# One core, attention and two MLPs: the written-out order of 1,198 steps is replaced by another order of the same steps

## The chip, the cores and the metric

The kernel runs on one core of a Trainium2 chip. The metric is the device time of one execution in microseconds (us). Lower is better. The engines are named as in the profile: PE is the matrix engine, PEld its weight loads, DVE the vector engine, ACT the scalar engine, POOL the GpSimd engine, and SP the queue that issues all loads and stores here.

## The reference

```python
# attention: q, k, v are (2, 8, 576, 64)
q_d = q.reshape(B, H, 144, 4, D).mean(axis=3)      # k_d, v_d alike
out_d = softmax_attention(q_d, k_d, v_d)           # scale 1/sqrt(D)
out_up = np.repeat(out_d, 4, axis=2)
mask = np.abs(pos[:, None] - pos[None, :]) < 4
out_local = softmax(where(mask, scale * q @ k.T, -1e9)) @ v
x = (out_up + out_local) -> (1152, 512)
# first MLP: w_in (512, 2048), w_out (2048, 512)
h = x @ w_in
x = where(h > 0, h, exp(min(h, 0)) - 1) @ w_out
# second MLP: 4 experts, w1 (512, 1024), w2 (1024, 512) each
p = probs / (probs.sum(-1) + 1e-9)
out = sum_e p[:, e] * (maximum(x @ w1[e], 0) @ w2[e])
```

The inputs of the first MLP's weights are 64-bit numbers, which the kernel converts itself from their two 32-bit words.

## The kernel before, in words

All products of the MLPs are done in three passes on numbers that are split into a high and a low part, so that a product step of the first MLP is 12 matmuls of 288 columns.

The attention and the first MLP are not a loop nest. They are cut into steps, and a string, `ORDER`, lists them. `run` takes the string token by token and issues each step's instructions. From then on nothing reorders them: each engine executes its own instructions in the order of the string, and an instruction that waits for another engine holds up all that stands behind it on its own engine. After the string comes the second MLP (`quad`, `l2e`), whose order a program merges; the change doesn't touch it.

A token is a name, its indices, and behind a colon an option: `:v`, `:a` or `:g` chooses DVE, ACT or POOL, and a number chooses how many products of nothing PE executes first. Those are matmuls of the identity with a column of zeros, 256 columns wide, into the step's own PSUM bank, which the step's real matmuls then overwrite (line 480). There are eight PSUM banks in a ring: a step that takes one waits until the step that held it has been read out.

The digit 0 or 1 in front of an attention step is the batch. The steps that the change and the prediction speak of:

- `LK`, `LV`, `VB`, `wF`, `mF`, `nF`: loads on the SP queue (queries and keys, values, slices of values, weights).
- `CP`: copies a loaded half of q or k into another layout (batch 0 only). `Tp`: PE transposes it (line 575). `Te`: DVE or ACT moves the result from PSUM to `qkT`.
- `PQ`: DVE sums `qkT` over groups of four into `pooled` (line 592). `PVa`, `PVb`: the same for v, on POOL.
- Local attention, nine blocks a batch: `LSp` scores (lines 621 and 625), `LSm` maximum (DVE, line 634), `LSx` exponentials (ACT), `LEr` and `LEm` normalise (line 661), `LTp` transposes (line 669), `LTe` moves, `LPp` multiplies by v (line 685), `LPa` adds the pooled part, `LPh` and `LPl` write the high and the low part of x (line 710).
- Pooled attention: `GSp` scores (line 722), `GSm`, `GSx`, `GEr`, `GEm` (line 764) the softmax, `GTp` transposes (line 776), `GTe` moves, `GPp` and `GPe` the product with v (line 799).
- Weights of the first MLP, in eight pieces a slice: `wA` (ACT), `wB`, `wC` (line 302), `wD` (line 309), `wE` (line 316) on DVE convert; `wH` (ACT) and `wL` (line 330, DVE or POOL) split.
- First MLP: `hp` product (line 264, `psH`), `ha`, `he` (ACT), `hd` (DVE), `hh` (ACT), `hl` (line 866, DVE or POOL); then `yp` product (line 264, `psY`) and `ya`, which adds it up.
- `m` and `n` steps prepare the first weights of the second MLP, and `xh`, `xl`, `xd`, `xth`, `xtl` its input. `W` is ten products of nothing at the start, and `C` closes the attention's memory.

Loaded tensors and split weights share nine slots of memory (`s8`). A load waits until the tensor that had its slot was used up, and loads behind it on SP wait too.

Of the kernel before, what the change touches and what calls it, by code (L numbers as in the profile page):

```python
# [1125 lines left out]
```

## Time and profile before

| | us |
|---|---|
| median of 3 runs | 672.08 |
| lowest and highest run | 671.48 and 673.28 |
| profiled execution | 674.41 |
| its span, from the first to the last instruction | 672.2 |

The profiled execution's time has 2.2 us outside its span. Its mean granted PE clock is 1.000. Busy times are from this one execution. A share of busy time is a mean over stages: the attention and the first MLP end at about 292 us of the span, and the second MLP takes the rest.

### The profile page before, as it was taken

How to read it: one execution, taken by the hardware profiler on the slowest of the kernel's cores; microseconds unless marked ns; L12 is line 12 of the kernel's file. 1: busy time of each engine (PE TensorE's matmuls, PEld its weight loads, DVE VectorE, ACT ScalarE, POOL GpSimd, SP SyncE). 2: the span in 40 equal slices, each digit the busy share in tenths (PEclk: the TensorE clock that was granted, in tenths of full speed). 3: DMA queues.
4: the chain of work that ended last, by engine and by line, in shares of the span. 5: the costliest groups of instructions: out<-in, count | busy, mean ns of one | idle time of the engine just before them, and what ended most of it. 6: DMA issues, size and time to landing. Idle time of an engine off the chain costs nothing.

```text
span 672.2 us, 12384 instructions
## 1 busy us (share of the span) xinstructions
PE 662.5 (99%) x4933; PEld 609.1 (91%) x4933; DVE 454.3 (68%) x893; ACT 298.7 (44%) x792; POOL 256.7 (38%) x226
## 2 busy tenths in 40 slices
...
DMA packets 40737, 46.71 MB, mean 69 GB/s; under 512 B 23015, under 2 KB 23015, under 8 KB 40679
## 3 DMA queue, kind: packets, MB, share of 16 engines
...
## 4 chain that ended last, share of the span: by engine, by line
PE 84%; DVE 10%; issue 2%; ACT 1%; POOL 1%; DMA 1%; DVEq 0%; ACTq 0%; POOLq 0%
PE psH L264 37%; PE psZ L264 29%; PE psY L264 13%; DVE raw L309 1%; DVE pooled L592 1%; PE psT L480 1%; DVE raw L316 1%; DVE w L330 1%; DVE cv L302 1%; DMA raw<-in_k_dram 1%; PE psP L669 1%; PE psGT L480 1%; DVE acc L920 1%; PE psS L625 1%; PE psGT L776 1%
## 5 line engine op out<-in xcount | busy, mean ns | idle before, releaser
L264 PE MATMUL psZ<-wr,h 128*128 128x512 f32 x864 | 199.2, 390 | 0.0
L264 PEld LDWEIGHTS psZ<-wr,h 128*128 128x128 f32 x864 | 161.3, 188 | 33.2
L1008 DVE TENSOR_TENSOR u<-psH,u 128x288 f32<-128x288 f32 x224 | 97.8, 454 | 30.6 <-PE psH L264 22.9
L1069 DVE SCALAR_TENSOR_TENSOR oacc<-psZ,pn,oacc 128x512 f32<-128x512 f32 x63 | 47.2, 750 | 96.3 <-PE psZ L264 96.3
L264 PE MATMUL psH<-x,w 128*128 128x288 f32 x768 | 109.1, 296 | 0.6 <-DVE x L710 0.4
L264 PE MATMUL psY<-g,w 128*128 128x288 f32 x768 | 108.2, 296 | 0.0
L264 PEld LDWEIGHTS psH<-x,w 128*128 128x128 f32 x768 | 103.5, 188 | 1.9 <-POOL x L710 0.6
L264 PEld LDWEIGHTS psY<-g,w 128*128 128x128 f32 x768 | 103.7, 188 | 0.5 <-issue 0.2
L1011 ACT ACTIVATE h<-u 128x288 fp32r<-128x288 f32 x128 | 56.5, 443 | 97.6 <-DVE u L1008 95.4
L1015 DVE SCALAR_TENSOR_TENSOR h<-u,h 128x288 fp32r<-128x288 f32 x128 | 88.5, 696 | 6.7 <-ACT h L1011 4.9
L264 PE MATMUL psH<-xt,ws 128*128 128x288 f32 x576 | 82.2, 295 | 0.3 <-POOL xt L930 0.3
L264 PEld LDWEIGHTS psH<-xt,ws 128*128 128x128 f32 x576 | 78.5, 188 | 0.5 <-POOL xt L930 0.5
L1025 ACT ACTIVATE u<-psH 128x288 f32<-128x288 f32 x32 | 12.9, 403 | 141.5 <-PE psH L264 141.5
L264 PE MATMUL psH<-xbo,wa 128*128 128x288 f32 x384 | 61.4, 295 | 0.0
L370 POOL TENSOR_TENSOR st<-raw 128x256 f32<-128x256 f32 x32 | 28.1, 880 | 77.9 <-DMA raw<-in_moe_w_dram 77.4
L264 PEld LDWEIGHTS psH<-xbo,wa 128*128 128x128 f32 x384 | 55.4, 188 | 1.2
L398 POOL TENSOR_TENSOR ws<-st,ws 128x1024 fp32r<-128x1024 f32 x16 | 38.7, 2417 | 44.7 <-ACT ws L392 44.7
L398 POOL TENSOR_TENSOR wa<-raw,wa 128x256 fp32r<-128x256 f32 (+1 forms) x32 | 34.5, 1082 | 45.4 <-ACT wa L392 45.4
L866 POOL TENSOR_TENSOR g<-gf,g 128x288 fp32r<-128x288 f32 x31 | 25.9, 845 | 59.6 <-ACT g L861 56.3
L436 POOL TENSOR_TENSOR wr<-raw,wr 128x1024 fp32r<-128x1024 f32 x16 | 39.5, 2486 | 18.8 <-ACT wr L431 18.8
L854 DVE SCALAR_TENSOR_TENSOR gf<-m,psH 128x288 f32<-128x288 f32 x64 | 28.2, 449 | 23.9 <-ACT m L849 12.7
L845 ACT ACTIVATE m<-psH 128x288 f32<-128x288 f32 x64 | 25.8, 403 | 26.6 <-PE psH L264 16.3
...
## 6 DMA issues: line engine op xcount, KB each, us to landing
raw<-in_moe_w_dram SPq DMA_DIRECT2D x16, 1024.0 KB, 5.2
raw<-in_moe_w_in_dram SPq DMA_DIRECT2D x8, 1024.0 KB, 6.0
raw<-in_moe_w_out_dram SPq DMA_DIRECT2D x8, 1024.0 KB, 6.7
...
```

The costliest lines, as they stand in the source:

```text
L264: nc.tensor.matmul(ps, wt[a], xt[b], start=first and n == 0, stop=last and n == 2)
L370: nc.gpsimd.tensor_tensor(out=st[:, o], in0=x, in1=y, op=op)
L398: nc.gpsimd.tensor_tensor(out=lo, in0=x, in1=hi.bitcast(F32), op=sub)
L436: nc.gpsimd.tensor_tensor(out=t[:, 1], in0=raw[0][:, 2 * j:2 * j + 2], in1=t[:, 0].bitcast(F32), op=ALU.subtract)
L480: nc.tensor.matmul(ps[:, :256], identb, junk.to_broadcast([P, 256]), start=True, stop=True)
L845: nc.scalar.activation(m, ps1["h", s, t, f][:, :HB], AF.Relu, scale=-1.0)
L854: nc.vector.scalar_tensor_tensor(out=gf, in0=m, scalar=-1.0, in1=ps[:, :HB], op0=ALU.add, op1=ALU.max)
L866: ENG[eng].tensor_tensor(out=g[:, 1], in0=gf, in1=g[:, 0].bitcast(F32), op=ALU.subtract)
L1008: nc.vector.tensor_tensor(out=o, in0=y, in1=x, op=ALU.add)
L1011: nc.scalar.activation(dest(i, k)[0], c, AF.Relu)
L1015: nc.vector.scalar_tensor_tensor(out=l, in0=c, scalar=0.0, in1=h.bitcast(F32), op0=ALU.max, op1=ALU.subtract)
L1069: nc.vector.scalar_tensor_tensor(out=a, in0=ps, scalar=sc, in1=a, op0=ALU.mult, op1=ALU.add)
```

## The change

The string `ORDER` is replaced by another with the same 1,198 steps: no step is added or left out. What differs is where each one stands, on which of two or three engines some of them run, and the products of nothing. Before, 14 steps have them, 121 in all; after, 13 steps, 129 in all. Nothing else in the program changes. The diff up to about the place of `1GTp.0.2`, and its last lines:

```diff
ORDER = """
-W 0LK.1.1 0CP.1.1.0:v 0Tp.1.2.0:5 0CP.1.1.1:v 0Tp.1.2.1 0Te.1.2.1:v 0Tp.1.3.0 0LK.0.0 0CP.0.0.1:v 0Tp.0.1.1:8
-0Tp.0.0.1 0CP.0.0.0:a 0LK.1.0 0CP.1.0.0:a 0CP.1.0.1:v 0Tp.1.1.1:12 0Tp.1.0.1 0Te.1.1.1:v 0Te.0.1.1:a 0Te.0.0.1:a
-0Tp.0.1.0 0Te.0.1.0:v 0Te.1.2.0:v 0LK.0.1 0CP.0.1.1:a 0Tp.0.2.1:12 0Te.0.2.1:a 0CP.0.1.0:a 0Tp.1.3.1 0Te.1.3.1:a
-0Tp.0.3.1 0Te.0.3.1:v 0Te.1.0.1:a 0Tp.1.0.0 0Te.1.0.0:a 0Te.1.3.0:v 0PQ.1.1 0Tp.0.3.0:6 0Te.0.3.0:v 0LV.0 0PVa.0
-0PVb.0 0Tp.0.2.0 0Te.0.2.0:a 0PQ.0.1 0Tp.1.1.0 0Te.1.1.0:a 0PQ.1.0 0Tp.0.0.0 0Te.0.0.0:a 0LSp.3:6 0LSm.3 0LSx.3
-0PQ.0.0 0LSp.4 0LSm.4 0LV.1 0PVa.1 0PVb.1 0VB.1 0GSp.0.1 0GSm.0.1 wF.0.1 wA.0.2 wB.0.2 wA.0.3 wB.0.3 wC.0.2
-wD.0.2 0GSx.0.1 0GEr.0.1 0GEm.0.1:g wF.0.2 0LSp.1 0LSp.6 0LSp.2 0LSm.2 0LSx.2 0LSm.1 0GSp.0.0 0GSm.0.0 0GSx.0.0
-wC.0.3 wD.0.3 wE.0.2 0GEr.0.0 0GEm.0.0:g 0GTp.0.2:30 0GTe.0.2:v 0LSp.0 0LSm.0 0GSp.1.0 0GSm.1.0 0LSx.1 0LEr.1
-0LEm.1:v 0LSx.4 0LEr.2 0LEm.2:g 0GTp.0.3 0GTe.0.3:a 0LSp.7:5 0LSm.7 0GTp.0.0:4 0GTe.0.0:v 0LTp.1:10 0LTe.1:v
-wA.0.4 wB.0.4 wF.0.0 wA.0.0 wB.0.0 wC.0.0 0GSx.1.0 0GEr.1.0 0GTp.0.1 0GTe.0.1:a 0LTp.3:12 0LTe.3:a 0LTp.4 0LSx.0
-wD.0.0 wA.0.1 wE.0.0 wH.0.0 0GEm.1.0:v 0LEr.0 0LPp.1 0GPp.0 0GPe.0:a 0LTe.4:a wH.0.2 wB.0.1 wC.0.1 0LSp.8 0LSm.8
-0LEm.0:g 0LPa.1 wD.0.1 0LPh.1 0LPl.1:g 0GTp.1.1 0GTe.1.1:a 1LK.0.0 1Tp.0.1.0 1Te.0.1.0:a 1Tp.0.3.0 1Te.0.3.0:a
-0LTp.2 0LTe.2:v 0LSx.7 0VB.4 0LPp.4:4 0LTp.0 0LTe.0:a 1VB.8 wL.0.0:v wE.0.3 wE.0.1 wH.0.1 0VB.2 0LPp.2 0LPa.2
-0LPh.2 wL.0.2:g 0VB.3 0LPp.3 0LPa.3 0LPh.3 1LK.1.0 1Tp.1.3.0 1Te.1.3.0:a 1Tp.1.2.0 1Te.1.2.0:v 0LPl.2:v 0LPl.3:g
-wL.0.1:g 1Tp.0.0.0 1Te.0.0.0:v 0LSx.8 0LPa.4 0LPh.4 0LPl.4:g 0LSp.5 0LSm.5 0VB.0 0LPp.0 0LPa.0 0LPh.0 0LSm.6
-0GSp.1.1 0GSm.1.1 0GTp.1.0 0GTe.1.0:a 1Tp.0.2.0 1Te.0.2.0:a 1Tp.1.1.0 1Te.1.1.0:a 1Tp.1.0.0 0LSx.5 0LPl.0:v
-hp.0.0.1 hp.0.0.0 wC.0.4 wD.0.4 0LEr.4 0LEm.4:v 0LTp.8 0LTp.7 wH.0.3 wL.0.3:v wF.0.3 wA.0.6 wB.0.6 wA.0.7 wB.0.7
-wC.0.6 wD.0.6 0LSx.6 0LEr.3 hp.0.0.2 0LEm.3:v wE.0.6 0GSx.1.1 0GEr.1.1 0LTp.6:2 hp.0.0.3 wE.0.4 ha.0.0.0
-he.0.0.0 hd.0.0.0 0LTp.5 0GEm.1.1:g ha.0.0.1 he.0.0.1 hd.0.0.1 0GTp.1.3:5 0VB.6 0LTe.6:v 0LPp.6 wC.0.7 wD.0.7
-wE.0.7 1VB.1 wA.0.5 wB.0.5 wC.0.5 0LTe.8:a 0GTp.1.2 hh.0.0.0 hh.0.0.1 hl.0.0.1:v hl.0.0.0:g 1Te.1.0.0:a 1LSp.0
-1LSm.0 0GTe.1.3:a 0LTe.5:a 0GTe.1.2:a ha.0.0.2 he.0.0.2 hd.0.0.2 0LTe.7:a 1LK.0.1 1Tp.0.1.1 1Te.0.1.1:a
-1Tp.0.2.1 1Te.0.2.1:a wD.0.5 wE.0.5 wH.0.4 hh.0.0.2 hl.0.0.2:g 0GPp.1 0GPe.1:a 0LPa.6 0VB.8 0LPp.8 0LPa.8 wF.1.0
-wA.1.0 wB.1.0 wC.1.0 0LPh.6 0LPl.6:v 0LPh.8 0LPl.8:v 0VB.7 0LPp.7 0LPa.7 wH.0.5 wL.0.5:g 0VB.5 0LPp.5 0LPa.5
-1Tp.0.0.1 1Te.0.0.1:a ha.0.0.3 he.0.0.3 hd.0.0.3 0LPh.7 0LPl.7:v 1LSp.3 1LSm.3 1LSp.1 1LSm.1 0LPh.5 0LPl.5:g
-hh.0.0.3 hl.0.0.3:v wD.1.0 wL.0.4:v 1LK.1.1 1Tp.1.2.1 1Te.1.2.1:a 1Tp.1.3.1 1Te.1.3.1:a 1Tp.1.1.1 1Te.1.1.1:a
-1Tp.1.0.1 1Te.1.0.1:a wF.1.3 wA.1.6 wB.1.6 wA.1.7 wB.1.7 wC.1.7 wD.1.7 wC.1.6 wD.1.6 wH.0.6 wL.0.6:g 1LSp.2
-1LSm.2 1Tp.0.3.1 1Te.0.3.1:a hp.0.1.0 ha.0.1.0 he.0.1.0 hd.0.1.0 hp.0.1.1 ha.0.1.1 he.0.1.1 hd.0.1.1 wH.0.7
-wL.0.7:v hp.0.1.2 ha.0.1.2 he.0.1.2 wE.1.7 1VB.3 hh.0.1.0 hl.0.1.0:v hd.0.1.2 hh.0.1.1 hl.0.1.1:g hp.0.1.3
-ha.0.1.3 he.0.1.3 hd.0.1.3 hh.0.1.2 hl.0.1.2:g hh.0.1.3 hl.0.1.3:g 1PQ.1.1 wF.1.2 wA.1.5 wB.1.5 wA.1.1 wB.1.1
-wC.1.1 wD.1.1 wE.1.1 1VB.6 yp.0.0.0 ya.0.0.0 wC.1.5 wD.1.5 1LSx.1 1LSp.4 1LSx.2 1LEr.1 yp.0.0.1 ya.0.0.1
-yp.0.1.0 ya.0.1.0 1LSx.0 wF.1.1 wA.1.2 wA.1.3 1LSm.4 wE.1.0 wH.1.0 wH.1.1 yp.0.0.2 ya.0.0.2 yp.0.1.1 ya.0.1.1
-1VB.2 yp.0.0.3 ya.0.0.3 1LEm.1:g 1LTp.1 1LTe.1:a 1LTp.2 1LSx.4 1LTe.2:a 1LSx.3 1PQ.0.1 1GSp.0.1 wB.1.3 wC.1.3
-wD.1.3 wE.1.3 wA.1.4 wL.1.1:v yp.0.1.2 ya.0.1.2 wL.1.0:v hp.1.0.0 ha.1.0.0 hp.1.0.1 he.1.0.0 ha.1.0.1 he.1.0.1
-1LV.0 wB.1.2 wC.1.2 wD.1.2 wE.1.2 wE.1.6 1LEr.2 1LEm.2:v 1LTp.4 1LTe.4:a 1LTp.3 1LEr.0 1LEm.0:g 1GSm.0.1
-1GSx.0.1 wB.1.4 1PQ.0.0 yp.0.1.3 ya.0.1.3 1PVa.0 1PVb.0 wH.1.2 wL.1.2:g wH.1.3 1PQ.1.0 hd.1.0.0 hh.1.0.0
-hd.1.0.1 hh.1.0.1 1LSp.6 1LSm.6 1LSx.6 1LSp.5 1LSm.5 1LSx.5 1GSp.0.0 1GSm.0.0 1GSx.0.0 1LTp.0 1LSp.7 1LSp.8
-wL.1.3:v hp.1.0.3 hp.1.1.3 1LSm.7 1LSx.7 hl.1.0.1:v 1GEr.0.1 1GEm.0.1:v 1GTp.0.2 1GTe.0.2:a 1GTp.0.3 1GTe.0.3:a
-wE.1.5 wC.1.4 wD.1.4 wE.1.4 1LPp.2 1LTe.3:a hp.1.0.2 1LSm.8 1LSx.8 hl.1.0.0:g 1GEr.0.0 1GEm.0.0:v 1GTp.0.0
...
-xh.2.1 yp.3.1.2 ya.3.1.2 yp.3.1.3 ya.3.1.3 xd.0.1 xh.1.3 xl.1.3:v xh.1.2 xl.1.2:v xd.0.2 xd.0.3 xth.0.2
-xtl.0.2:v xth.0.3 xtl.0.3:v xth.0.1 xtl.0.1:v xh.2.2 xl.2.2:g xl.2.1:g yp.3.3.0 ya.3.3.0 yp.3.3.1 ya.3.3.1
-yp.3.3.2 ya.3.3.2 yp.3.3.3 ya.3.3.3 xh.3.2 xl.3.2:v xh.3.3 xl.3.3:v
+W 0LK.1.0 0CP.1.0.0:v 0Tp.1.0.0:5 0CP.1.0.1:a 0Tp.1.1.1 0Te.1.1.1:v 0Tp.1.0.1 0Te.1.0.1:v 0Te.1.0.0:v 0Tp.1.1.0
+0Te.1.1.0:v 0PQ.1.0 0LK.1.1 0CP.1.1.1:a 0CP.1.1.0:a 0Tp.1.3.0:15 0Te.1.3.0:v 0Tp.1.3.1 0Te.1.3.1:v 0Tp.1.2.1
+0Te.1.2.1:v 0LK.0.1 0CP.0.1.0:a 0CP.0.1.1:v 0Tp.0.3.0:4 0Te.0.3.0:v 0Tp.0.2.0 0Te.0.2.0:v 0LK.0.0 0CP.0.0.1:a
+0Tp.0.1.1:10 0Tp.0.0.1 0CP.0.0.0:a 0Tp.0.0.0:2 0Te.0.1.1:a 0Tp.0.1.0 0Te.0.0.1:a 0Te.0.0.0:v 0Tp.1.2.0
+0Te.1.2.0:v 0PQ.1.1 0Te.0.1.0:a 0PQ.0.0 0Tp.0.2.1 0Te.0.2.1:a 0LV.0 0PVa.0 0PVb.0 0LV.1 0PVa.1 0PVb.1 0Tp.0.3.1
+0Te.0.3.1:a 0LSp.1 0LSm.1 0LSx.1 0PQ.0.1 0LSp.2 0LSm.2 0LSp.3 0LSm.3 0GSp.0.1:23 0GSm.0.1 0LSp.4 0LSp.8 wF.0.1
+wA.0.3 wB.0.3 wA.0.2 wB.0.2 wC.0.3 wC.0.2 wD.0.3 wD.0.2 0GSp.0.0 0GSm.0.0 0LSx.3 0LSx.2 0LEr.1 0GSx.0.1 0GEr.0.1
+wF.0.0 wA.0.0 wB.0.0 wA.0.1 0GSx.0.0 0LSp.0 0LSm.0 0VB.3 0GSp.1.0:5 0LSm.4 0LSx.4 0GEm.0.1:g 0GTp.0.2:30
+0GTe.0.2:a 0GTp.0.3 0GTe.0.3:a 0GSm.1.0 0GSx.1.0 0LSp.5 wC.0.0 0GEr.0.0 wB.0.1 0GEm.0.0:v 0GTp.0.0:6 0GTe.0.0:a
+0GTp.0.1 0GTe.0.1:a 0LEr.2 0LEm.1:v 0LTp.1:5 0LTe.1:a 0LTp.2 0LSx.0 0LTe.2:a 0GPp.0 0GPe.0:a 0LEm.2:v 0LTp.3
+0LTe.3:a 0LTp.4 wD.0.0 0GEr.1.0 wE.0.0 wH.0.0 0GEm.1.0:v 0GTp.1.1 0GTe.1.1:a wC.0.1 0LEr.0 wE.0.3 wE.0.2 wH.0.2
+0LSm.5 0VB.1 0LPp.1 0LPa.1 0LPh.1 0LTe.4:a 0VB.5 0LPp.3 0LPa.3 0LPh.3 0GTp.1.0 0GTe.1.0:v 0LEm.0:g 0LTp.0:9
+0LTe.0:a wL.0.0:g 0LSm.8 1LK.0.0 1Tp.0.2.0 1Te.0.2.0:a 1Tp.0.3.0 1Te.0.3.0:a 1Tp.0.0.0 1Te.0.0.0:a wD.0.1 wE.0.1
+wH.0.1 0LPl.3:v wH.0.3 0LSp.7 0LSm.7 0VB.2 0LPp.2 0LPa.2 0LPh.2 0LPl.1:g wF.0.3 wA.0.6 wL.0.2:v wL.0.3:v 0LSx.8
+0LPl.2:v wL.0.1:g 0VB.0 0LPp.0 0LPa.0 0LPh.0 0LPl.0:g 0LSp.6 0LSm.6 0VB.4 0LPp.4 0LPa.4 0GSp.1.1 0GSm.1.1
+1LK.1.0 1Tp.1.0.0:4 1Tp.1.2.0 1Tp.1.1.0 1Te.1.2.0:v 1Te.1.1.0:v 1Tp.0.1.0:11 0LPh.4 0LPl.4:g hp.0.0.0 wB.0.6
+wC.0.6 wD.0.6 0LSx.7 hp.0.0.2 0LEr.4 0GSx.1.1 0GEr.1.1 0GEm.1.1:v 0GTp.1.3 0GTp.1.2 0LEm.4:v wF.0.2 wA.0.5
+wB.0.5 wA.0.4 wB.0.4 wC.0.4 wD.0.4 wC.0.5 wE.0.4 0LSx.6 0LSx.5 0LEr.3 wD.0.5 0GTe.1.2:a 0LEm.3:g 0GTe.1.3:a
+ha.0.0.0 he.0.0.0 hd.0.0.0 hp.0.0.1 ha.0.0.1 he.0.0.1 hd.0.0.1 0LTp.8 0LTe.8:v wE.0.5 wA.0.7 wB.0.7 wC.0.7
+hh.0.0.0 hl.0.0.0:v hh.0.0.1 hl.0.0.1:v hp.0.0.3 ha.0.0.3 he.0.0.3 0GPp.1 0GPe.1:a wD.0.7 wH.0.4 wL.0.4:g 0LTp.6
+0LTe.6:a 1Te.0.1.0:a 0LTp.7 0LTe.7:a 0LTp.5 0VB.8 0LPp.8 0LPa.8 0LTe.5:a 0LPh.8 0VB.6 0LPp.6 0LPa.6 hd.0.0.3
+wE.0.7 1Tp.1.3.0 1Te.1.3.0:a 0LPh.6 0LPl.6:v 1LK.1.1 1Tp.1.2.1 1Tp.1.1.1 1Tp.1.0.1 1Te.1.0.1:a 1Tp.1.3.1
+1Te.1.3.1:a 1Te.1.2.1:v 0LPl.8:g 0LPp.5 0LPa.5 wE.0.6 0VB.7 0LPp.7 0LPa.7 1Te.1.0.0:a 1LSp.2 1LSp.1 1LSp.0
+1LSm.2 ha.0.0.2 he.0.0.2 hd.0.0.2 0LPh.5 0LPl.5:g 0LPh.7 0LPl.7:v hp.0.1.0 hp.0.1.1 hp.0.1.2 hp.0.1.3 wH.0.5
+wL.0.5:v hh.0.0.2 hl.0.0.2:v hh.0.0.3 hl.0.0.3:v wF.1.0 wA.1.0 wB.1.0 wC.1.0 wD.1.0 wE.1.0 wH.0.6 wL.0.6:v
+wH.0.7 wL.0.7:g ha.0.1.0 he.0.1.0 hd.0.1.0 yp.0.0.0 1Te.1.1.1:a 1LSp.4 1LSm.1 ha.0.1.1 he.0.1.1 hd.0.1.1
+yp.0.0.1 wF.1.1 wA.1.2 wB.1.2 wC.1.2 wD.1.2 wE.1.2 wA.1.3 wB.1.3 wC.1.3 wD.1.3 1LSx.2 hh.0.1.0 hl.0.1.0:v
+hh.0.1.1 hl.0.1.1:v 1LSx.1 1LEr.1 1LEm.1:g ha.0.1.3 he.0.1.3 hd.0.1.3 ha.0.1.2 he.0.1.2 hd.0.1.2 hh.0.1.2
+hl.0.1.2:g hh.0.1.3 hl.0.1.3:g 1LK.0.1 1Tp.0.2.1 1Tp.0.0.1 1Te.0.2.1:v 1Te.0.0.1:a 1Tp.0.1.1 1Te.0.1.1:a 1PQ.1.1
+wA.1.1 1LSp.3 1LSm.3 1LSx.3 wB.1.1 wC.1.1 wD.1.1 wE.1.1 yp.0.0.2 ya.0.0.2 1LSm.0 1Tp.0.3.1 1Te.0.3.1:a 1PQ.0.1
+wH.1.0 wL.1.0:g wH.1.1 wL.1.1:g 1VB.8 1LSm.4 yp.0.1.0 ya.0.1.0 1LTp.2 1LTe.2:a 1LSp.5 1LSm.5 ya.0.0.0 wF.1.3
+wA.1.7 wB.1.7 wA.1.6 wB.1.6 wC.1.7 wC.1.6 wD.1.7 1LTp.1 1LSx.0 1LEr.0 1LEm.0:g 1LTe.1:a 1GSp.0.1 1GSm.0.1
+1GSx.0.1 wD.1.6 wE.1.6 yp.0.1.1 ya.0.1.1 1PQ.0.0 1LV.0 1PVa.0 1PQ.1.0 hp.1.0.0 ha.1.0.0 he.1.0.0 hd.1.0.0
+hp.1.0.1 ha.1.0.1 he.1.0.1 hd.1.0.1 wF.1.2 wA.1.5 wB.1.5 wA.1.4 wB.1.4 wC.1.5 wD.1.5 wE.1.3 1LSx.4 1LEr.2
+1LEm.2:v ya.0.0.1 wH.1.2 wL.1.2:v wH.1.3 wL.1.3:g yp.0.1.2 ya.0.1.2 1LTp.0 1LSx.5 1LTe.0:v yp.0.1.3 hh.1.0.0
+hh.1.0.1 ya.0.1.3 1GSp.0.0 1GSm.0.0 1GSx.0.0 1LSp.6 1LSm.6 1LSx.6 yp.0.0.3 ya.0.0.3 1LSp.8 1LSm.8 1LTp.4
+hp.1.0.2 ha.1.0.2 he.1.0.2 1LTp.3 1LSx.8 hp.1.1.0 ha.1.1.0 1VB.1 1LPp.1 1LTe.4:a hp.1.0.3 1PVb.0 wC.1.4 wD.1.4
+wE.1.4 wE.1.5 1GEr.0.0 hl.1.0.1:v hd.1.0.2 hh.1.0.2 hl.1.0.0:g 1GEr.0.1 1GEm.0.1:v 1GTp.0.2 1GTe.0.2:a 1GTp.0.3
+1GTe.0.3:a 1GEm.0.0:v 1GTp.0.0 1GTe.0.0:v 1GTp.0.1 1GTe.0.1:a 1VB.0 1LPp.0 1LTe.3:v 1LV.1 1PVa.1 1PVb.1 1LSp.7
...
+yp.3.1.3 ya.3.1.3 xh.1.3 xd.0.1 xl.1.3:v xh.1.2 xl.1.2:v xd.0.2 xth.0.2 xd.0.3 xtl.0.2:v xth.0.3 xtl.0.3:v
+xth.0.1 xtl.0.1:g yp.3.3.0 ya.3.3.0 yp.3.3.1 ya.3.3.1 yp.3.3.2 ya.3.3.2 xh.3.2 xl.3.2:g yp.3.3.3 ya.3.3.3 xh.3.3
+xl.3.3:v
```

## Rows read from the trace of the kernel before

**Rows 1.** The page's first part: busy us, share of the span, instructions.

```profile
PE 662.5 (99%) x4933; PEld 609.1 (91%) x4933; DVE 454.3 (68%) x893; ACT 298.7 (44%) x792; POOL 256.7 (38%) x226
```

**Rows 2.** Busy time by stretch: length, then PE, PEld, DVE, ACT, POOL, clock, DMA.

```profile
20.00:40.00 20.00, 18.88 (x280) 15.79 (x280) 18.71 (x48) 15.19 (x73) 5.42 (x6) 1.00 1.05 198
...
80.00:100.00 20.00, 18.97 (x182) 17.02 (x182) 19.42 (x38) 17.82 (x73) 6.81 (x6) 1.00 0.12 32
```

**Rows 3.** The chain of work that ended last: start, us, what.

```profile
25.97 3.49 PE psGT L480 x30
...
93.50 1.04 PE psP L669 x8
...
107.54 0.88 DVE aT L473 x2
...
128.71 0.44 PE psP L669 x4
...
130.77 1.58 PE psH L264 x12
```

**Rows 4.** Timeline of DVE: start, us, line, operation, output and input.

```profile
22.36 1.34 DVE L592 TENSOR_REDUCE pooled<-qkT 128x288 f32<-128x1152 f32 x1
...
102.28 0.76 DVE L764 TENSOR_TENSOR eg<-eg,gsm 80x576 f32<-80x576 f32 x1
```

**Rows 5.** PE by line and shape, 0 to 13 us: busy us, mean ns.

```profile
L480 PE MATMUL psT<-junk,identb 128*128 128x256 bf16 x21 | 4.9, 413 | 1.1 <-DVE identb L971 1.1
```

**Rows 6.** DVE by line and shape, 20 to 103 us: busy us, mean ns, idle before.

```profile
L309 DVE SCALAR_TENSOR_TENSOR raw<-raw,cv 128x512 uint32<-128x512 uint32 x15 | 11.8, 786 | 0.4
L316 DVE SCALAR_TENSOR_TENSOR raw<-raw 128x512 uint32<-128x512 uint32 x15 | 11.1, 750 | 0.2
...
L302 DVE TENSOR_SCALAR cv<-cv 128x512 uint32<-128x512 uint32 x15 | 6.6, 443 | 0.3
...
L330 DVE TENSOR_TENSOR w<-raw,w 128x512 fp32r<-128x512 f32 x7 | 4.7, 683 | 0.0
...
L473 DVE COPY pT<-psP 70x512 f32<-70x512 f32 x3 | 2.0, 678 | 0.7 <-PE psP L669 0.7
L866 DVE TENSOR_TENSOR g<-gf,g 128x288 fp32r<-128x288 f32 x4 | 1.8, 449 | 0.0
```

**Rows 7.** Waits of DVE, 18 to 104 us: total, times, longest.

```profile
DVE pT L473 <- PE psP L669: 0.7, 1, 0.7
```

**Rows 8.** Timeline of PE.

```profile
38.06 1.33 PE L799 MATMUL psO<-aT,vp 72*64 72x80 f32 x32
39.32 0.30 PE L621 MATMUL psS<-masks,identb 128*128 128x280 bf16 x1
...
40.16 0.49 PE L776 MATMUL psGT<-ident,eg 64*72 64x64 f32 x4
...
43.34 1.15 PE L685 MATMUL psX<-pT,vb 70*64 70x64 f32 x32
...
46.77 0.71 PE L722 MATMUL psG<-pooled 64*64 64x144 f32 x8
...
103.80 0.72 PE L776 MATMUL psGT<-ident,eg 80*72 80x80 f32 x8
...
292.06 0.96 PE L264 MATMUL psH<-xbo,wa 128*128 128x288 f32 x6
```

**Rows 9.** Waits of PE over the whole span.

```profile
PE psGT L480 <- ACT eg L744: 1.0, 1, 1.0
```

**Rows 10.** Lines 316 and 710: duration in ns, least, median, most.

```profile
L316 DVE SCALAR_TENSOR_TENSOR raw<-raw x32: 652/693/2857, 29.6 to 247.9; 128x512 uint32<-128x512 uint32 x32
...
L710 POOL TENSOR_TENSOR x<-xf,x x9: 720/741/3074, 42.0 to 147.0; 128x256 fp32r<-128x256 f32 x9
```

**Rows 11.** DMA issues: line, count, KB, us from issue to landing.

```profile
raw<-in_moe_w_out_dram SPq DMA_DIRECT2D x8, 1024.0 KB, 6.7
```

106 lines of the change are left out of this document (53 added, 53 removed).

## The prediction

> **What bounds the kernel now.** I read the page's first part, then busy time by stretch, then the chain of work that ended last. The page says that PE is busy 662.5 of 672.2 us [rows 1]: over the whole span there is little left to win. The stretches say something else for the first sixth. From 20 to 100 us, DVE is busy 18.7 to 19.4 of each 20 us (the first and last of four rows), PE no more than that, and PE's time there holds products of nothing and matmuls spread thin [rows 2]. The chain of waits decides between the two: up to 93.50 us it runs mainly through DVE, with pieces such as the 30 products at 25.97 us between, and from there mainly through PE, broken once more by DVE pieces that begin at 107.54 us [rows 3]. Behind that, as at 128.71 and 130.77 us, the pieces are PE's own [rows 3]. So a new order can win only in two ways: by bringing DVE sooner to where PE takes over, and by leaving PE fewer waits behind that. The second MLP (from 292 us) is PE at its pace and is not touched; I take it as unchanged.
>
> **The marker.** I measure at the step `1GTp.0.2`, which needs DVE's `1GEm.0.1`. Before, that multiply starts at 102.28 and takes 0.76 us, so it ends at 103.04 [rows 4], and PE starts `1GTp.0.2` at 103.80 [rows 8].
>
> **The front, to 24 us.** Before, the fourth pooling sum `PQ` is started at 22.36 us and ends at 23.70, at 1.34 us each [rows 4]; all four stand behind the last evacuations on DVE. After, `PQ.1.0` stands behind the first four transposes, where DVE has nothing else: 1.3 us less behind the last evacuation. PE has 36 products among the sixteen transposes where it had 43, and the 20 of them at the very start are 25 before. Early products take 4.9 us for 21, 0.23 us each, at a mean of 413 ns [rows 5], against 3.49/30 = 0.12 us later [rows 3]: PE runs at the lower of its two levels (1.2 GHz) there. So PE's part is 5 x 0.23 + 2 x 0.12 = 1.4 us shorter. Whether that moves DVE depends on the loads of q and k, of which the order is changed but not the number. Bounds: -2.7 us (both) and 0. I take -1.7: the sum, and a quarter of PE's part.
>
> **A new wait.** After, `0GSp.0.1` stands behind 23 products, and `0GSm.0.1`, next on DVE but for two maxima, waits for its scores. 23 x 0.12 = 2.7 us behind three score blocks, against 0.44-us-sized work on DVE: by my count of both queues DVE stands idle 1.3 us. Queued behind it are the weight conversions `wB` to `wD` and then `GEr.0.1`, for which POOL and `GTp.0.2` wait. Bounds 0 and 2.7; I take +1.3.
>
> **More work on DVE ahead of the marker.** I counted each queue's steps ahead of `1GTp.0.2` in both strings, behind the front. DVE gets one more each of `wC`, `wD`, `wE` (0.44 + 0.79 + 0.75), three more `hl` (3 x 0.45), two `GEm` that POOL had (2 x 0.76, [rows 4]) and two more evacuations of the 0.44 us of line 473 [rows 3, 6]; it loses two `wL` (2 x 0.68), one `LTe` (0.68) and one `LPl` (taken as another split, 0.45). Sum: 1.98 + 1.35 + 1.52 + 0.88 - 1.36 - 0.68 - 0.45 = +3.2 us [rows 6]. POOL's queue is about as long as before, ACT's 2 us longer, and ACT isn't full. Bounds: 2.7 (these overlap by some 0.08 us at their ends) and 3.2.
>
> **A wait that goes.** DVE waited 0.7 us for PE once, in `LTe` behind a transposition with ten products [rows 7]. `0LTe.1` is on ACT after, and the products are five: -0.7. So DVE is at the marker at -1.7 + 1.3 + 3.2 - 0.7 = +2.1 us.
>
> **What PE has done by then.** Ahead of the marker the new string has one `hp` more (1.58, [rows 3]), one `LPp` more (1.15/2 = 0.58, [rows 8]) and one `LSp` less (40.16 - 39.32 = 0.84, [rows 8]): 1.3 us of real work less is left. +2.1 - 1.3 = +0.8 us.
>
> **Behind the marker.** Before, from 103.80 to 292.06 us [rows 8] PE has 188.3 us. The work in it: 52 `hp` and 56 `yp` at 1.58 [rows 3], 170.6; 4 `LTp` at 0.44 [rows 3], 8 `GTp` at 0.72/2, 9 `LPp` at 0.58, 2 `GPp` at 1.33, 2 `GSp` at 0.71 [rows 8], together 13.9. 188.3 - 184.5 = 3.8 us of waits, most in the DVE pieces from 107.54 us on. After, by the same sums of queues, DVE, ACT and the banks' releases come ahead of PE everywhere behind the marker, by half a microsecond at the least and mostly by more than 2. I leave 0.8 us. Bounds: 0 and 3.8. That is -3.0 us, and the sum is 0.8 - 3.0 = **-2.2 us**.
>
> **At nothing.** The products from the first `LSp` on are 93 for 78: 15 x 0.12 = 1.8 us. I cost them at nothing, as the marker is DVE's and they fill PE's waits ahead of it; without that cover they cost 1.8. Before, one wait ahead of the 30 products cost PE 1.0 us besides [rows 9]. Loads: the same number on SP. `wF.1.2` now waits for a slot that POOL's `wL.1.1` frees, and `1LV.0` stands ahead of it; a load of its kind takes 6.7 us to land [rows 11], about what there is until `wA.1.5`. A late one delays ACT, which has several microseconds to spare: 0, bound 1.
>
> **The clock.** From 20 to 100 us the granted clock is 1.00 in every stretch [rows 2], so there is no lower level to win back there.
>
> **Forecast.** The profiled execution's 672.2 us of span with 2.2 around them gives 674.4; the runs' median is 672.08, 2.3 lower, and I set the change against it: 672.08 - 2.2 = **669.9 us**. A difference of 0.3%, 2.0 us, is about what can be told from none.
>
> **Rivals.**
>
> *The gain is used up ahead of the marker* (no change). The front brings only `PQ`'s 1.3 us and half the old waits stay behind the marker (2.0 for 0.8): -2.2 + 0.4 + 1.2 = -0.6, 671.5 us. For it: DVE has 3 us more to do in the stretch that binds. Against: PE's waits behind 107 us have their cause in steps that now stand earlier.
>
> *POOL holds DVE up* (slower). Line 316 takes 693 ns and once 2857; POOL's line 710 takes 741 and once 3074 [rows 10]. One such meeting costs DVE 2.2 us. More `wL` of 1.3 us and a `LPl` go to POOL ahead of the marker, between DVE's two-input steps. Two more meetings, +4.4, give 674.3; it decides from 4.2 us of added DVE time. Against: `GEm` and `hl` leave POOL, and its queue gets no longer. The Trainium skill (SBUF — State Buffer, "SBUF: two separate sides") calls the ports that the two share an exclusive lock: whoever starts first keeps it for the whole instruction. By that rule, such long steps are waits for the lock, and the two maxima agree.
>
> *The clock falls* (slower). A wait of about 2 us for the bank of `1Tp.0.1.0`, longer than the 1.0 us that PE waited before [rows 9], takes PE to 1.2 GHz. At 0.23 for 0.12 us a product, 4 us at that level cost 2 and set back what follows: about 673.
>
> *DVE loses less* (much faster). DVE's idle time from 20 to 100 us (3.2 us by four rows, [rows 2]) halves and the new wait vanishes: -2.2 - 1.6 - 1.3 = -5.1, 667.0 us.
>
> **How the numbers follow.** Forecast 0.43 (its own range 668 to 670), much faster 0.10, used up 0.32, POOL 0.12, clock 0.03. So faster 0.53, same 0.32, slower 0.15. The range from 666.5 to 672.8 leaves out the slow end and the last of the fast one.
>
> **What would show it.** `1GEm.0.1` ends 1 to 4 us later than 103.04, and yet PE's pieces from 107 us on have no DVE pieces between them: the steps are right. PE passes into the second MLP at about 289.9 us, not 292.06. A DVE idle of about 1.3 us stands near 22 us, in front of the pooled maximum. Wrong would be: the chain staying in DVE behind 110 us, more two-input DVE steps above 2 us, a granted clock below 1.00 between 20 and 292 us, or a second MLP of another length.

## The result, and the profile after

The changed kernel took 681.97 us, the median of 4 runs (681.03 to 683.74), and the kernel before 672.68 beside it (671.48 to 673.88): a ratio of 1.014, with a 95% interval of 1.0125 to 1.0162. I had forecast 669.9 us, with 672.8 as the upper end. The order makes the kernel 9.3 us slower. The profiled execution took 681.8 us at a span of 680.0; line numbers are one higher than before.

The page's first part, against [rows 1]: PE is as busy as ever, and 4.7 us more.

```profile
PE 667.2 (98%) x4941; PEld 613.0 (90%) x4941; DVE 458.8 (67%) x890; ACT 300.5 (44%) x795; POOL 256.4 (38%) x226
```

Busy time by stretch, against [rows 2]: length, then PE, PEld, DVE, ACT, POOL, granted clock, DMA.

```profile
20.00:40.00 20.00, 19.82 (x284) 16.59 (x281) 18.95 (x49) 18.89 (x79) 5.12 (x5) 1.00 1.15 220
...
80.00:100.00 20.00, 18.35 (x171) 16.25 (x170) 19.30 (x34) 14.80 (x54) 9.79 (x7) 1.00 0.40 104
100.00:120.00 20.00, 16.84 (x146) 15.18 (x146) 14.62 (x26) 11.80 (x43) 3.96 (x4) 0.74 0.27 52
```

Two numbers stand out. POOL is busy 9.79 us from 80 to 100 where it was busy 6.81. And from 100 to 120 us PE is busy 16.84, at a mean granted clock of 0.74: with two levels, 1.2 and 2.4 GHz, that is (1 - 0.74) x 2 x 20 = some 10 us at the lower one.

PE's waits over the whole span, against [rows 9]: what PE waited for, total, times, longest.

```profile
PE psGT L777 <- DVE eg L765: 3.2, 1, 3.2
PE psT L481 <- DVE qkT L474: 1.2, 1, 1.2
...
PE psH L265 <- DVE gf L855: 0.6, 1, 0.6
```

The 3.2 us are the marker's: PE waits in `1GTp.0.2` for `1GEm.0.1`. PE's timeline says when, and when the second MLP starts, against [rows 8].

```profile
103.61 1.85 PE L265 MATMUL psH<-x,w 128*128 128x288 f32 x12
108.61 2.33 PE L777 MATMUL psGT<-ident,eg 80*72 80x80 f32 x16 [3.15 <-DVE eg L765]
...
113.40 1.12 PE L686 MATMUL psX<-pT,vb 70*64 70x64 f32 x16
114.45 5.38 PE L265 MATMUL psH<-x,w 128*128 128x288 f32 x24
...
122.86 0.69 PE L686 MATMUL psX<-pT,vb 70*64 70x64 f32 x16
...
299.37 0.96 PE L265 MATMUL psH<-xbo,wa 128*128 128x288 f32 x6
```

`1GTp.0.2` starts at 108.61 us (103.80 before), the second MLP at 299.37 (292.06 before). The two profiled spans differ by 7.8 us: 4.8 up to the marker, 2.5 from there to the second MLP and 0.5 in it. The medians differ by more, 9.3, mainly because the execution that was profiled before took 674.41 us, 1.7 above the median. Behind the idle stretch the 24 matmuls from 114.45 us take 5.38 us, where the 12 of their kind ahead of it take 1.85; 16 products of line 686 take 1.12 us, and 0.69 from 122.86 on. The chain of waits names the steps that made `1GEm.0.1` late, against [rows 3]: start, us, what.

```profile
96.54 1.78 DVE w L331
...
104.62 1.94 DVE gsm L756
...
106.79 1.69 DVE eg L765
...
108.61 2.33 PE psGT L777 x16
```

The chain stays in DVE until 108.5 us, where I had it in PE from 107 on, and its DVE pieces are longer than they ought to be: 1.78 us for a step of 0.69, 1.94 for one of 0.16, 1.69 for one of 0.75. DVE's and POOL's timelines side by side, against [rows 4], show what each long step has next to it: start, us, engine, line.

```profile
17.23 2.35 POOL L602 TENSOR_TENSOR vtmp<-vraw 72x1024 f32<-72x1024 f32 x1
17.36 1.34 DVE L593 TENSOR_REDUCE pooled<-qkT 128x288 f32<-128x1152 f32 x1
...
86.36 2.98 POOL L602 TENSOR_TENSOR vtmp<-vraw 72x1024 f32<-72x1024 f32 x1
...
87.10 2.78 DVE L317 SCALAR_TENSOR_TENSOR raw<-raw 128x512 uint32<-128x512 uint32 x1
...
96.37 1.41 POOL L331 TENSOR_TENSOR w<-raw,w 128x512 fp32r<-128x512 f32 x1 [7.04 <-issue]
96.54 1.78 DVE L331 TENSOR_TENSOR w<-raw,w 128x512 fp32r<-128x512 f32 x1
...
104.15 2.37 POOL L602 TENSOR_TENSOR vtmp<-vraw 72x1024 f32<-72x1024 f32 x1 [3.94 <-DMA vraw<-in_v_dram]
104.16 0.45 DVE L855 SCALAR_TENSOR_TENSOR gf<-m,psH 128x288 f32<-128x288 f32 x1 [0.20 <-ACT m L850]
...
104.54 2.01 DVE L756 TENSOR_SCALAR gsm<-gsm 80x4 f32<-80x4 f32 x1
...
106.59 1.26 POOL L607 TENSOR_TENSOR vp<-vtmp 72x512 f32<-72x512 f32 x1
106.79 2.35 DVE L765 TENSOR_TENSOR eg<-eg,gsm 80x576 f32<-80x576 f32 x2
```

Four times a DVE step that began while a two-input step of POOL was running ended only behind that step. `wE.1.6` (line 317) starts at 87.10; POOL's `1PVa.0` ends at 86.36 + 2.98 = 89.34, and `wE.1.6` at 89.88. `wL.1.2` ends 0.54 us behind POOL's `wL.1.3`. The scale in `1GEr.0.1` (line 756), on 80x4 numbers, ends at 106.55, and `1PVa.1` at 106.52. `1GEm.0.1` ends 0.6 us behind `1PVb.1`. The four took 2.78 + 1.78 + 2.01 + 1.68 = 8.25 us where 0.69 + 0.69 + 0.16 + 0.75 = 2.29 are usual: 6.0 us. Line 855, which reads one operand from a PSUM bank and not from SBUF, the memory that holds the other steps' operands, took its usual 0.45 at 104.16, under the same `1PVa.1`. That is the rule of the Trainium skill (SBUF — State Buffer, "SBUF: two separate sides"): an exclusive lock between the two engines, held for the whole instruction. The trace agrees to 0.6 us at each of the four places.

### The profile page after: what moved, and what is told of

Read it like the earlier page. It is cut to its first block, busy times and chain, and to the rows that moved or that the text cites. A ratio compares the mean times of both kernels' runs of the same rounds, so it can differ in the third digit from the quotient of the medians.

```text
span 680.0 us, 12419 instructions
## 1 busy us (share of the span) xinstructions
PE 667.2 (98%) x4941; PEld 613.0 (90%) x4941; DVE 458.8 (67%) x890; ACT 300.5 (44%) x795; POOL 256.4 (38%) x226
## 4 chain that ended last, share of the span: by engine, by line
PE 82%; DVE 3%; ACT 1%; POOL 0%; issue 0%; DVEq 0%; ACTq 0%
PE psH L265 38%; PE psZ L265 29%; PE psY L265 13%; PE psX L686 1%; PE psGT L777 1%; DVE raw L310 0%; PE psO L800 0%; DVE gsm L756 0%; DVE cv L297 0%; PE psP L670 0%; POOL xt L931 0%; DVE w L331 0%; DVE raw L317 0%; DVE eg L765 0%; ACT eg L745 0%
## 5 line engine op out<-in xcount | busy, mean ns | idle before, releaser
L265 PE MATMUL psH<-x,w 128*128 128x288 f32 x768 | 111.1, 299 | 1.2 <-DVE gf L855 0.6
L265 PEld LDWEIGHTS psH<-x,w 128*128 128x128 f32 x768 | 105.7, 191 | 2.4 <-DVE gf L855 0.9
L399 POOL TENSOR_TENSOR wa<-raw,wa 128x512 fp32r<-128x512 f32 (+1 forms) x32 | 34.6, 1085 | 40.8 <-ACT wa L393 40.8
L867 POOL TENSOR_TENSOR g<-gf,g 128x288 fp32r<-128x288 f32 x28 | 23.5, 846 | 57.7 <-ACT g L862 57.5
L331 POOL TENSOR_TENSOR w<-raw,w 128x512 fp32r<-128x512 f32 x14 | 20.0, 1432 | 53.3 <-ACT w L326 46.2
```

Source lines behind the costliest of these rows:

```text
L265: nc.tensor.matmul(ps, wt[a], xt[b], start=first and n == 0, stop=last and n == 2)
L331: ENG[eng].tensor_tensor(out=t[:, 1, r], in0=up.bitcast(F32), in1=t[:, 0, r].bitcast(F32), op=ALU.subtract)
L399: nc.gpsimd.tensor_tensor(out=lo, in0=x, in1=hi.bitcast(F32), op=sub)
L867: ENG[eng].tensor_tensor(out=g[:, 1], in0=gf, in1=g[:, 0].bitcast(F32), op=ALU.subtract)
```

## The experiments

**28 products ahead of the marker** (e1_products), to part the cost of the clock from that of the wait.

```diff
-1GTp.0.2
+1GTp.0.2:28
```

> The changed kernel with 28 products of nothing ahead of 1GTp.0.2, the step for which TensorE stood idle 3.2 us before its granted clock fell to 0.5 (1.2 GHz) for 10.2 us. Nothing else is changed, so 1GEm.0.1 ends as late as before (108.5 us). Theory 'the clock': the idle stretch took the clock down, and the lower level costs 4 to 4.5 us of the 9.3 us lost; with the products the granted clock stays at 1.00 from 100 to 125 us and the time falls to 677.2 to 678.5 us, although 1GTp.0.2 starts no sooner than 108.6. Rival 'late work': the steps behind 108 us wait for VectorE's late results anyway, so a faster TensorE only waits longer there: 681 to 682 us with the clock at 1.00.

Measured: 679.45 us, the median of 6 runs (676.92 to 682.48), ratio 1.0097 (1.0065 to 1.0130). Busy time by stretch:

```profile
40.00:60.00 20.00, 18.60 (x226) 16.40 (x225) 17.24 (x41) 16.21 (x64) 4.09 (x4) 0.91 0.69 155
100.00:120.00 20.00, 19.11 (x226) 16.75 (x223) 17.53 (x31) 13.81 (x53) 7.20 (x6) 1.00 0.30 55
```

From 100 to 120 us the clock stays at 1.00. From the first transposition of `1GTp.0.2` to the second MLP it is 298.16 - 111.62 = 186.5 us, for 299.37 - 108.61 = 190.8 without the products: the lower level cost **4.2 us**, and no later wait gave any of it back. The median came down less than forecast because in some executions, the profiled one among them, the clock fell elsewhere: between 40 and 60 us, around a wait of 1.2 us for a bank in `1Tp.0.1.0`. The marker is 3.0 us later in this profile. The changed kernel has the same wait and kept its clock there in its profile; the kernel before has no such wait. Three of the six runs have a mean granted clock of 1.00 and took 676.9 to 678.8 us, about what the theory has; three have 0.995 to 0.997 and took 680.1 to 682.5.

**1PVa.1 behind 1GEm.0.0** (e2_pool_later), to take away one meeting and nothing else.

```diff
-                raw = self.vraw[half]
+                raw = self.vraw[half]; self.opt and nc.gpsimd.tensor_copy(tmp[0:1, 0, 0:1], self.eg[0, 0][0][0:1, 0, 0:1])
...
-1PVa.1
+1PVa.1:e
```

> The changed kernel with one edit on GpSimd: ahead of 1PVa.1 it copies one element of the product that VectorE's 1GEm.0.0 has made, so that its two sums (2.4 and 1.3 us) begin behind that step and not at 104.15 us. Theory 'GpSimd holds VectorE up': the two-number scale in 1GEr.0.1 goes back from 2.01 to 0.17 us and 1GEm.0.1 from 1.68 to 0.75, 1GEm.0.1 ends at about 105.7 (108.47), TensorE waits 0.5 us in place of 3.2, the granted clock stays at 1.00, and the time is 674 to 676 us (2.8 of the wait and 4 to 4.5 of the clock gone from 682). Rival 'VectorE simply has more to do': the steps take as long as they did, 1GEm.0.1 ends behind 107.5, and the time is within 1 us of the changed kernel's 682.

Measured: 675.25 us (10 runs, 674.31 to 675.96), ratio 1.0038 (1.0024 to 1.0052). DVE's, PE's and POOL's timeline:

```profile
104.90 0.16 DVE L756 TENSOR_SCALAR gsm<-gsm 80x4 f32<-80x4 f32 x1
...
105.30 1.42 DVE L765 TENSOR_TENSOR eg<-eg,gsm 80x576 f32<-80x576 f32 x2
106.20 1.42 PE L777 MATMUL psGT<-ident,eg 80*72 80x80 f32 x16 [0.38 <-DVE eg L765]
106.89 0.17 POOL L600 COPY vtmp<-eg 1x1 f32<-1x1 f32 x1 [6.33 <-ACT g L862]
107.15 2.36 POOL L602 TENSOR_TENSOR vtmp<-vraw 72x1024 f32<-72x1024 f32 x1
```

The scale takes 0.16 us again and the two `1GEm` 1.42 together. `1GTp.0.2` starts 2.4 us sooner, PE's wait is 0.38 for 3.15, and the clock stays up. 2.4 and the clock's 4.3 (292.68 - 106.20 = 186.5 us to the second MLP) make 6.7 us, and 681.97 - 675.25 is 6.7. The theory holds and its rival falls: DVE had the same steps to do.

**Three places of the order** (e3_reorder), against the two earlier meetings.

```diff
-wD.1.6 wE.1.6 ... 1PVa.0 ... hd.1.0.1 ... wL.1.3:g ... 1PVb.0
+wD.1.6 ... 1PVa.0 1PVb.0 ... hd.1.0.1 wE.1.6 ... wL.1.3:v
```

> The changed kernel with three places of its order changed so that GpSimd's two-input steps meet VectorE's less, and nothing added: wE.1.6 behind hd.1.0.1 (it took 2.78 us at 87.10, under 1PVa.0), 1PVb.0 right behind 1PVa.0, and wL.1.3 on VectorE in place of GpSimd (0.69 us more for it; wL.1.2 took 1.78 beside it). Theory 'GpSimd holds VectorE up': wE.1.6 and wL.1.2 go back to 0.69 us, 1GEm.0.1 then ends near 102.5, that is before 1PVa.1's data are there, so this meeting goes too; TensorE reaches 1GTp.0.2 without a wait of over 1 us, the clock stays at 1.00, and the time is 671.5 to 674.5 us. Rival 'VectorE simply has more to do': 1GEm.0.1 ends behind 106 us, and the time stays within 1.5 us of 682.

Measured: 679.29 us (4 runs, 679.17 to 679.38), ratio 1.0098 (1.0069 to 1.0127): neither forecast. DVE's, POOL's and PE's timeline:

```profile
102.38 2.35 POOL L602 TENSOR_TENSOR vtmp<-vraw 72x1024 f32<-72x1024 f32 x1 [4.87 <-DMA vraw<-in_v_dram]
102.42 0.17 DVE L759 RECIPROCAL gsm<-gsm 80x4 f32<-80x4 f32 x1
102.63 4.46 DVE L765 TENSOR_TENSOR eg<-eg,gsm 80x576 f32<-80x576 f32 x2
104.81 1.66 POOL L607 TENSOR_TENSOR vp<-vtmp 72x512 f32<-72x512 f32 x1
105.49 1.21 PE L777 MATMUL psGT<-ident,eg 80*72 80x80 f32 x8 [2.16 <-DVE eg L765]
```

The two meetings are all but gone (`wE.1.6` takes 0.83 us, `wL.1.2` and `wL.1.3` together 1.29), and `1GEm.0.1` starts at 102.63 us, 4.2 sooner. I had taken it for granted that `1PVa.1` would still begin at 104.15. But its load waits for a slot that DVE's own `wL` steps free: SP issues it at 96.43 us, right behind them, where it was 98.40. So it landed sooner too: POOL began at 102.38 and caught both `1GEm`, 4.46 us for 1.42. PE waits 2.16 us for the first, and its clock falls again: from `1GTp.0.2` to the second MLP it takes 296.70 - 105.49 = 191.2 us. A meeting can't be cured by being earlier, if what one meets hangs on the same engine and comes earlier too.

**Both together** (e5_reorder_later): the three places and the gate.

```diff
-1PVa.1
+1PVa.1:e
```

> The changed kernel with the edits of the last two runs together: the three places of the order, and 1PVa.1 begun only behind 1GEm.0.0. In the run with the three places alone, 1GEm.0.1 started at 102.63 us and met 1PVa.1, which its own data had let start at 102.38: 1.96 us lost there, 1.06 more in 1GEm.0.0, TensorE idle, and the clock down for 10.24 us. Theory 'GpSimd holds VectorE up, then the clock falls': with both meetings gone 1GEm.0.1 ends at about 103.4, TensorE, which has ended hp.1.0.3 at 103.3, goes on with a wait below 0.5 us, the clock stays at 1.00, and the time is 671.5 to 673.5 us, level with the kernel before. Rival 'another wait takes its place': 1GTp.0.2 starts behind 105 us, 674 to 676.

Measured: **672.58 us** (12 runs, 671.89 to 673.36), ratio 0.9989 (0.9978 to 1.0000). `1GTp.0.2` starts at 103.86 us with a wait of 0.21, and the granted clock stays at 1.00. With no step added or left out but one copied element, the loss is gone. Of the 9.4 us to the changed kernel's 681.97, 2.4 lay in the meeting at the marker and 4.3 in the clock behind it. The 2.7 that are left go with the two earlier meetings: without them `1GTp.0.2` starts 2.3 us sooner than with the gate alone.

**The fault put into the kernel before** (e4_before_pool2, and e4_before_pool1 with one).

```diff
+            def PX(self):
+                nc.gpsimd.tensor_tensor(out=self.ptmp, in0=self.ptmp, in1=self.ptmp, op=ALU.add)
...
-hl.1.0.0:g
+hl.1.0.0:g 1PX 1PX
```

> The kernel before with the fault put in: two sums of the size of 1PVa (72x1024, 2.4 us each) are added on GpSimd right behind hl.1.0.0 (100.6 us), on a buffer that 1PVa.1 writes anew later. Nothing on any other engine is added or moved, and GpSimd has nothing else to do until 107 us. Theory 'GpSimd holds VectorE up, then the clock falls': hl.1.0.1, 1GEr.0.1 and 1GEm.0.1 stretch by about 3.7 us together, 1GEm.0.1 ends at about 106.7 (103.04), TensorE stands idle 3 us or more at 1GTp.0.2, its granted clock falls to 0.5 for some 10 us behind it, and the time is 677 to 681 us. Without the fall of the clock it is 675 to 676.5. Rival 'the two engines don't touch each other': 672 to 673 us.

> The kernel before with one added sum of 72x1024 on GpSimd behind hl.1.0.0, where the earlier run had two (679.7 us). Theory 'GpSimd holds VectorE up': hl.1.0.1 alone stretches, by 1.3 us or so, and what stands behind it on VectorE is as much later; 1PVa.1 began 0.3 us behind the end of 1GEm.0.0 before, so now 1GEm.0.0 or its 1GEr meets it and loses 2 us more. TensorE then waits for 1GTp.0.0: 675 to 677 us if its clock stays at 1.00, 678 to 680.5 if it falls. Rival 'the loss is in proportion to what is added': half of the 6.8 us that two cost, 676, with no meeting at 1GEm.0.0. Rival 'no lock': 672 to 673.

Measured with two: 679.67 us (4 runs, 679.05 to 681.42), ratio 1.0108 (1.0076 to 1.0141). DVE's and POOL's timeline:

```profile
98.51 4.47 POOL L605 TENSOR_TENSOR vtmp<-vtmp 72x1024 f32<-72x1024 f32 x2
99.45 1.78 DVE L869 TENSOR_TENSOR g<-gf,g 128x288 fp32r<-128x288 f32 x1
101.16 1.85 DVE L758 TENSOR_SCALAR gsm<-gsm 80x4 f32<-80x4 f32 x1
...
105.18 2.71 POOL L601 TENSOR_TENSOR vtmp<-vraw 72x1024 f32<-72x1024 f32 x1 [2.19 <-DMA vraw<-in_v_dram]
105.71 2.74 DVE L316 SCALAR_TENSOR_TENSOR raw<-raw 128x512 uint32<-128x512 uint32 x1
```

Work on an engine that had nothing else to do makes DVE's steps 1.78 for 0.45, 1.85 for 0.16 and, as a consequence at `1PVa.1`, 2.74 for 0.69. PE then waits twice in `GTp`, 3.7 us in all, and its mean granted clock from 100 to 120 us is 0.66. PE's timeline, and the stretch:

```profile
104.15 1.04 PE L779 MATMUL psGT<-ident,eg 80*72 80x80 f32 x8 [2.34 <-DVE eg L767]
...
106.18 3.25 PE L264 MATMUL psH<-x,w 128*128 128x288 f32 x12
110.74 1.26 PE L779 MATMUL psGT<-ident,eg 80*72 80x80 f32 x8 [1.31 <-DVE eg L767]
```

```profile
100.00:120.00 20.00, 16.35 (x138) 14.99 (x137) 16.85 (x25) 10.65 (x38) 9.30 (x6) 0.66 0.25 55
```

So the forecast time came in another way than I had it: not one wait of 3 us or more, but two. The clock falls behind the first, of 2.34 us, and is 0.50 from 104.5 to 118 us: the 12 matmuls from 106.18 us already take 3.25 us, where 1.85 are usual. The second wait lies within that stretch. It comes from a meeting that the first had brought on: `1PVa.1` starts 1.2 us behind the end of `1GEm.0.1`, where it was 4.2 in the kernel before.

With one sum: 676.79 us (10 runs, 672.49 to 678.25), ratio 1.0045 (1.0022 to 1.0067). The median lies in the range that I had for a clock that stays up, but that is luck, since it hides two groups. Three runs have a mean granted clock of 0.999 or 1.000 and took 672.5 to 673.5 us, seven have 0.992 to 0.996 and took 675.5 to 678.3. The profile fell on one of the three: `hl.1.0.1` alone is stretched, and `1PVa.1` starts 0.2 us behind `1GEm.0.0`'s start, so that no second meeting comes. What differs in the seven was not profiled; that `1PVa.1` comes ahead of `1GEm.0.0` in them is only argued.

**The front without products** (e6_front_bare), on the kernel of e5.

```diff
-0Tp.1.0.0:5 ... 0Tp.1.3.0:15 ... 0Tp.0.3.0:4 ... 0Tp.0.1.1:10 ... 0Tp.0.0.0:2
+0Tp.1.0.0 ... 0Tp.1.3.0 ... 0Tp.0.3.0 ... 0Tp.0.1.1 ... 0Tp.0.0.0
```

> The last kernel but one (three places of the order, 1PVa.1 behind 1GEm.0.0) without the 36 products of nothing among its first sixteen transpositions; those from the score blocks on stay. In the changed kernel the transpositions and products run at 0.12 us each from 6.9 us on, in the kernel before only from about 12.5, where TensorE had waited 1.1 us before its first transposition. Theory 'the clock makes the front': without the products TensorE waits for its copies between the transpositions, the double pace comes later than 9 us, the last of the four pooling sums ends 1.5 us or more behind 18.7 us, and the time is 1 to 3 us above the kernel with the products. Rival 'the order of the copies makes the front': the products only fill waits; the last pooling sum ends within 0.7 us of 18.7 and the time is within 1 us of the kernel with them.

Measured: 673.23 us (10 runs, 672.45 to 676.42) beside 672.58 with them. Busy time by stretch, and DVE's timeline:

```profile
0.00:20.00 20.00, 15.80 (x153) 11.12 (x154) 12.03 (x22) 8.38 (x20) 9.33 (x23) 0.74 0.93 256
```

```profile
16.41 1.34 DVE L593 TENSOR_REDUCE pooled<-qkT 128x288 f32<-128x1152 f32 x1
...
21.27 0.82 DVE L733 TENSOR_REDUCE gmx<-psG 80x2 f32<-80x288 f32 x2 [2.80 <-PE psG L723]
```

My theory was wrong for this part of the front. The clock is lower without the products (0.74 over the first 20 us, 0.50 from 9 to 14; the trace has the granted clock only from its first rise on, at 4.3 us here and 5.8 with them, and what stands ahead of that counts as 1.00), and yet the last pooling sum ends at 17.75 us, 0.9 sooner than with them (18.60). So it is not PE's pace that makes this part. Behind it DVE without the products waits 2.80 us for the scores, in place of 0.9, and the start is lost again. Taken together the products are worth 0.65 us by the medians, within the rival's 1 us and with runs that overlap.

**The front alone** (e9_front_alone): the first 64 steps of the changed order, then the order before.

```diff
-W 0LK.1.1 0CP.1.1.0:v 0Tp.1.2.0:5 ... 0GSp.0.1 0GSm.0.1
+W 0LK.1.0 0CP.1.0.0:v 0Tp.1.0.0:5 ... 0GSp.0.1:23 0GSm.0.1
```

> The kernel before with the changed kernel's first 64 steps (through 0GSm.0.1), and from there its own order with its own products; nothing of the later change is in it. In the changed kernel 0GSm.0.1 starts at 20.3 us in place of 24.0. Theory 'the front is a gain that later steps use up': alone it carries 2.5 to 3.5 us to 1GTp.0.2 (103.80 before), and the time is 669 to 670.5 us. Rival 'what stands behind takes it back': the 30 products at 0GTp.0.2 and the waits behind them absorb it, 671.5 to 673 us. Rival 'a meeting': the earlier steps meet GpSimd's long sums or 1PVa.1 at other places, 674 us or more.

Measured: 671.95 us (12 runs), ratio 0.9998 (0.9986 to 1.0010): the rival. The longest of DVE's waits, 18 to 30 us:

```profile
DVE cv L297 <- ACT cv L293: 1.4, 1, 1.4
```

The gain runs into the next thing: DVE stands 1.4 us in front of `wB.0.2`, whose weights land only at 23.1 us by the chain of waits. In the profiles not all of the gain is used up: the last pooling sum ends at 19.38 us, 4.3 sooner than in the kernel before, and `1GTp.0.2` starts at 102.22, 1.6 sooner. But the execution profiled before was 2.3 us above the median of 672.10 that the kernel before has beside this run, so the two profiles can't say where the rest goes; the medians say that nothing is left.

**A kernel faster than both** (e7_best, then e8_best2), on the kernel of e5.

```diff
-wB.0.0 ... 0LSm.0 ... 0LSm.4        wE.0.2 ... 0LPa.3    wL.0.2:v wL.0.3:v ... 0LPa.0
+0LSm.0 ... 0LSm.4 wB.0.0            0LPa.3 wE.0.2        0LPa.0 wL.0.2:v wL.0.3:v
-0GTp.0.2:30    wL.0.7:g    wD.3.5 wE.3.5 ... hd.3.2.0    0GSm.1.1 ... 1Te.1.2.0:v
+0GTp.0.2:20    wL.0.7:v    hd.3.2.0 wD.3.5 wE.3.5        1Te.1.2.0:v 0GSm.1.1
```

The last pair is e8_best2's alone.

> A try at a kernel faster than both: that of the first run of this call with six further edits of its order, each against a meeting or a wait seen in the trace: wB.0.0 behind 0LSm.4 (1.40 us for 0.42 beside a GpSimd product), wE.0.2 behind 0LPa.3 (1.15 for 0.69), wL.0.2 and wL.0.3 behind 0LPa.0 (1.57 for 0.69), wL.0.7 on VectorE (wE.1.0 took 1.69 beside it), 20 products for 30 at 0GTp.0.2 (-1.2 us of TensorE), and wD.3.5 and wE.3.5 behind hd.3.2.0, for which TensorE waited 0.8 us at 260 us. Theory: 0.8 us at 260 us for certain, and about 1 us more at 1GTp.0.2, which VectorE and TensorE reach together: 669.5 to 671.5 us. Rival 'a new meeting or a fallen clock eats it': one of the shifted steps meets GpSimd elsewhere, or TensorE waits behind the fewer products: 672 us or more.

> The last kernel of the earlier call with one more step moved: 0GSm.1.1 behind 1Te.1.2.0 on VectorE. That kernel's profile shows TensorE waiting 2.3 us for a bank ahead of 1Tp.0.1.0, which 1Te.1.2.0 frees, and its clock at 0.5 from 46.1 us for 3.4 us; its runs lay between 670.0 and 673.4. Theory 'the wait takes the clock down in some executions': with the wait gone the granted clock is 1.00 from 10 us to the end in every execution, TensorE is 1 us earlier at 1Tp.0.1.0, and the time is 669.5 to 670.8 us with a spread below 2 us. Rival 'the spread has another source': 671 to 671.7 us, and runs between 670 and 673.4 again.

Measured: e7_best 671.35 us (12 runs, 670.01 to 673.43), ratio 0.9981 (0.9966 to 0.9996); e8_best2 **670.47 us** (12 runs, 669.28 to 673.32), ratio 0.9975 (0.9961 to 0.9989). The wait at 260 us is gone in both. e8_best2 is the fastest kernel here, by 0.25% of the kernel before; the interval leaves out no difference, but the difference is small. That it is faster than e7_best is not shown: the kernel before took 672.65 us beside e7_best and 672.10 beside e8_best2. The wait for the bank in `1Tp.0.1.0` (1.2 us in e7_best's profile, not the 2.3 of the expectation) is gone as well, but not every fall of the clock. In e7_best four of the twelve runs have a mean of 0.997 and took 672.8 to 673.4; in e8_best2 two, the profiled one among them, have 0.995 and took 672.5 and 673.3. So the spread has, at least in part, another source, as the rival has it. In the profile the clock fell at the end of this stretch:

```profile
56.00:60.00 4.00, 3.81 (x68) 3.26 (x68) 4.00 (x7) 3.28 (x10) 2.22 (x2) 0.98 0.20 25
```

PE has no wait above 0.2 us from 40 to 70 us. What took the clock down, in a stretch of transpositions and 64-row matmuls, stays open.

## Why the prediction was wrong

It was wrong in sign. The step that failed is the sum for **DVE at the marker**, +2.1: it takes DVE's steps at their usual durations and has no term for POOL's hold on them. I had left that to the rival **POOL holds DVE up**, at 0.12, on the argument that "its queue gets no longer". The length of POOL's queue doesn't count; what counts is which DVE step is on when a POOL sum starts. The rival's mechanism was right, and its size was short: I allowed two more meetings, +4.4 us. From the last pooling sum to `1GEm.0.1` DVE's steps exceed the usual duration of their kind by some 4 us before and some 10 after: +6.2 to +6.4, by what is taken as usual. (Each step's duration less that of its kind without company, summed over 172 and 180 steps.) And its price had no second part: **the clock falls** stood apart from it, at another place and with 0.03, while the one brought on the other.

The rival also read one of its two maxima the wrong way round. Line 316's 2857 ns is DVE, held up by a POOL product at 210.4 us. Line 710's 3074 ns is POOL, held up by DVE, whose steps beside it keep their usual time (two of line 316 in 1.28 us). The hold works in both directions, and only the first costs DVE time. From the kernel before:

```profile
42.05 3.07 POOL L710 TENSOR_TENSOR x<-xf,x 128x256 fp32r<-128x256 f32 x1 [1.50 <-ACT x L705]
...
43.24 1.28 DVE L316 SCALAR_TENSOR_TENSOR raw<-raw 128x512 uint32<-128x512 uint32 x2
```

Point by point, on the profiled executions:

- *The front, -1.7 (-2.7 to 0).* The last pooling sum ends at 18.71 us for 23.70: -5.0, outside my bounds. I had priced all early work of PE at the lower pace; after, the products of the first 13 us take 280 ns at the mean where it was 413 [rows 5]:

```profile
L481 PE MATMUL psT<-junk,identb 128*128 128x256 bf16 x36 | 5.0, 280 | 0.4 <-DVE identb L972 0.4
```

  But PE's pace is not what my bounds lacked: in e6_front_bare the clock is lower and the sum ends sooner still. What is left, by exclusion, is the order of the loads and copies, for which I had no term. Part of the 5.0 is the profiled execution's own. The same first steps, in the two kernels with sums put in, end their last pooling sum at 22.26 and 20.50 us; so this front wins 1.8 to 5.0 us, by the execution that it is compared with.
- *A new wait, +1.3.* 0.9 us, in front of `0GSm.0.1`, where I put it.
- *More work on DVE, +3.2.* The usual durations of the steps behind the front add up to some 85 us for some 81.5: +3.2 to +3.5. Right, though one `hd` (0.45 us) and one `GEr` more stood nowhere in my sum.
- *A wait that goes, -0.7.* It is gone from DVE's waits; against [rows 7] the 0.9 us above stands first.

```profile
DVE gmx L733 <- PE psG L723: 0.9, 1, 0.9
```

- *DVE at the marker, +2.1.* 108.47 - 103.04 = +5.4. Without the stretched steps it would have been about -0.9, by subtraction: the front's larger gain and the missed meetings have opposite signs, and the second is the larger.
- *PE's work done, -1.3, and behind the marker, -3.0.* In e5, where no meeting and no clock disturbs it, PE takes 290.39 - 103.86 = 186.5 us from `1GTp.0.2` to the second MLP, for 188.3 before [rows 8]: -1.7, where the two terms promised -4.3. With the 1.3 us less of work that I counted, waits fell by 0.4, not by 3.0. There was no 3.0 to win. My 3.8 us of waits was a small difference of two large sums, while the trace has PE busy 187.4 of these 188.3 us before, and one wait above 0.1:

```profile
PE psX L685 <- DVE od L473: 0.8, 1, 0.8
```

  And the 0.8 that I left for after took no account of POOL, whose steps also stretch DVE at 250 to 260 us (two steps of line 297 take 990 ns at the mean there, for some 420 alone), so that PE waits 0.6 us more for line 855. e7_best took that wait away.
- *At nothing.* What the 15 products more cost was not tested by itself. The loads were not free: the slot that frees `1LV.1` sooner or later (SP issues it at 98.40 us, before at 101.30) decides when `1PVa.1` starts, and that is the largest item of the case. I had asked only whether a load comes late, not what it starts.
- *The clock.* "Nothing to win back" was true, and beside the point: it could be lost. It cost 4.3 us at the marker. The rival's own place, `1Tp.0.1.0`, saw falls too, in the profiled executions of e1_products and e7_best, around a wait of 1.2 us and not 2.
- *The second MLP.* 680.0 - 299.37 = 380.6 us for 380.1: unchanged, as taken.

Without the meetings, then, the order would have brought not the forecast but the first rival, *the gain is used up* (671.5): e5 is at 672.58, the kernel before at 672.65.
